# A new order of products, output steps and loads in the steady part of a convolution and SwiGLU kernel

## The chip, the core and the metric

The kernel runs on one core of a Trainium2 chip. The core has a matrix engine (TensorE, PE in the profile), a vector engine (VectorE, DVE), an engine for activations (ScalarE, ACT), a general one (GpSimd, POOL) and SyncE (SP), whose queue issues most of the transfers here. Each engine takes its instructions in order and waits on semaphores for the others. On-chip data lie in SBUF; TensorE writes to PSUM, which is held here as four double banks of 128 partitions by 1024 numbers. The metric is the device time of one execution in microseconds, from runs of the same program; a profiled execution gives the trace.

## The reference

A causal convolution of 7 taps over 8 sequences of 4096 tokens with 192 channels (8 heads share softmaxed taps), then an RMS norm and a SwiGLU feed-forward with 1536 inner channels, all in float32:

```python
out = np.einsum('hk,bskhg->bshg', w, x_unf)      # x_unf: 7 shifted copies of x
xn = x / rms * rms_g
g = xn @ w_gate
silu = g * (1.0 / (1.0 + np.exp(-g)))
val = xn @ w_val
return (silu * val @ w_out)
```

Almost all the work is three products per token, 192 x 1536 twice and 1536 x 192 once.

## The kernel before, in words

**Pairs.** The 32768 tokens are cut into 32 pairs of two groups of 512 tokens. Pair 0 and the first half of pair 1 are computed by plain products while the weights are converted. From pair 2 on every pair runs in the same way, and that is the steady part.

**Products.** The inner channels are cut into six blocks (0 to 5) of two 128-channel parts, so that a pair and a block make a 2 x 2 problem of cells a, b, c, d (group by part). Blocks 0, 2, 4 and 5 use the seven products of Strassen and Winograd (P1 to P7, with Q1 to Q4 as corrections); blocks 1 and 3 use twelve direct ones (A, B, E for each cell). A product is six matmuls of 512 columns in a split float32 format (`product`, L920). Together there are 68 a pair. Gate and value stand in the two halves of a double bank. Cells b, c and d of a Strassen block are put together from banks: f1 copies a to b, f3 copies c to SBUF, f4 and f5 add them (L991).

**Weights of the products.** The 48 pieces of weights a pair needs (192 KB each) don't fit in SBUF. They stand in DRAM (`wd`) and pass through a ring of ten slots. `ring_load` is called by the last product that uses a slot, and issues on SP's queue the load of the next piece of the list into that slot. The list is the order in which products first use the pieces, so the n-th load follows the (n-10)-th release. The c and d products of blocks 1 and 3 share three pieces: each set stays in the ring from its first to its second use. R starts the ring; its buffer is lent before that to the tokens of pair 2.

**Gates.** For each cell ScalarE makes the Silu of the gate (words ga to gd, L997) and VectorE multiplies it by the value (ma to md, L1004) into a cell of the hidden layer.

**Steps.** The output product is a 2 x 2 problem over two halves of the inner channels, again by Strassen and Winograd. For each block four sums of cells are made first (h1 to h4, L974, on VectorE or GpSimd), which overwrite cells: h2 may overwrite a cell only when step o1 of its block has read it, h4 only after o2. A step o*form.block* is one block's share of one of seven products in tiles of 32 columns (`step`, L947, 6 instructions in the program, 12 in the trace). There are 42 a pair. They gather in banks X, Y and Z; c1, c2 and s7 copy a bank on ScalarE; C22 and C21 (L1021) add two results on VectorE. o3 adds to the bank that C22 has to have read. T11, T12, T21, T22 (L962) transpose the results, and `leave` stores them (words st, ten a pair).

**Next pair.** The tokens of a later pair are loaded (ld), convolved by seven taps (cv0 on ScalarE, the others on VectorE, L455), squared, summed, scaled on GpSimd (sq, red, pow, bc, mul), put to DRAM in another layout (pl) and fetched back (ft). Four sums x1 to x4 (L842) and, for each of five operands, a split in three parts follow: n on ScalarE (L685), l on VectorE or GpSimd (L828), d on VectorE (L830).

**Order.** All of it is written out by hand. LINE is TensorE's order for one pair. ORDER is a list of words for one turn of the loop: p4 emits four entries of LINE; other words name the engine (V, A, G, S for VectorE, ScalarE, GpSimd and SP) and the operation; a plus or a minus after a word means the next pair or the one before. FIRST is the turn for pair 1. An engine runs its own words in the order given and takes no notice of how they mix with others.

Of the kernel before, what the change touches and what calls it, by code (L numbers as in the profile page):

```python
# [20 lines left out]
def kernel(  # L21
# [36 lines left out]
    PAIRS = B * NB  # L58
# [18 lines left out]
        "a5 b5 c5 d5",  # L77
    )
    ORDER = (
# [30 lines left out]
    )  # L110
    LINE = (
# [18 lines left out]
    x_sb = {}  # L130
# [31 lines left out]
    def load_part(p, h, eng):  # L162

        if h == 0:
            x_sb[p] = xs.tile([P, TB + HALO, GS], F32, name="xh")
        load_head(p, p // NB, (p % NB) * PT, h, eng)
# [219 lines left out]
    scr = {}  # L386
# [459 lines left out]
    class Pair:  # L846
# [81 lines left out]
        def step(self, form, k):  # L928
            b = ACC[form]
# [130 lines left out]
    def put_away(p, h, eng):  # L1060
        if h == 0:
            scr[p] = dram.tile([D, PT], F32, name="xd")
# [248 lines left out]
```

## Time and profile before

| what | value |
|---|---|
| runs | 2467.02 us median of 3 (2466.46 to 2467.69) |
| the profiled execution | 2466.55 us; its span 2464.8 us |
| granted TensorE clock | 0.999 |
| TensorE busy | 2449.7 us (99%) |
| VectorE busy | 2025.1 us (82%) |
| ScalarE busy | 1017.7 us (41%) |
| GpSimd busy | 835.0 us (34%) |
| DMA | 430.55 MB, mean 175 GB/s |

How to read it: busy time is the sum over which an engine had an instruction at work; the span runs from the first to the last instruction. The chain of waits follows the last instruction back, at each step to what released it. A timeline row is start, length, engine, line, operation, tiles and shapes, a count, and in brackets the idle time before it and who ended it. A window row gives for a stretch the busy time of TensorE, its weight loads, VectorE, ScalarE and GpSimd, then the granted clock, the share of the DMA engines and GB/s. Line numbers are those of the kernel before; in the changed one they are 23 or so higher.

### The profile page before, as it was taken

The numbers are of one execution on the slowest core, as the hardware profiler recorded it, in microseconds if no ns is written. First come the engines' busy times: TensorE is split into PE (matmuls) and PEld (weight loads), VectorE is DVE, ScalarE is ACT, GpSimd is POOL, SyncE is SP. The second block draws the span as 40 slices with busy tenths as digits, with TensorE's granted clock in tenths as the row PEclk, the third lists the DMA queues.
The fourth block names the chain that finished last, engine by engine and source line by source line (L and its number), as shares of the span: only waits on it lengthen the run. The fifth ranks groups of instructions, "written<-read, shape, count | busy, mean of one in ns | idle before, by whom it ended". The sixth has DMA issues, their size and how long they took to land.

```text
span 2464.8 us, 69197 instructions
## 1 busy us (share of the span) xinstructions
PE 2449.7 (99%) x29136; PEld 1892.1 (77%) x29136; DVE 2025.1 (82%) x2530; ACT 1017.7 (41%) x1431; POOL 835.0 (34%) x624
## 2 busy tenths in 40 slices
PE   8999999999999999999999999999999999999999
PEld 5647777778877777777788777777877777787777
DVE  8688878888888889888888888888887898888874
ACT  6443434433344434344334344334444343443332
POOL 0541333423343333333323334233433333333222
PEclk9999999999999999999999999999999999999999
DMA  7374678666778666676666786666786666776653
GB/s 152 61 209 133 175 179 206 185 178 164 170 196 205 175 170 171 172 204 184 194 159 176 180 210 182 177 165 170 195 205 179 165 172 173 202 187 194 159 162 95
DMA packets 716392, 430.55 MB, mean 175 GB/s; under 512 B 510330, under 2 KB 702386, under 8 KB 716082
## 3 DMA queue, kind: packets, MB, share of 16 engines
q1 hardware_dynamic: 712336, 425.21, 66.6%
q8 instruction: 230, 3.77, 0.7%
q10 hardware_dynamic: 3746, 0.92, 0.2%
q14 instruction: 80, 0.66, 0.1%
HBM read 366.96 MB, written 58.98 MB: 173 GB/s over the span
## 4 chain that ended last, share of the span: by engine, by line
PE 95%; DMA 2%; DVE 1%; SPq 1%; ACT 0%; issue 0%; POOL 0%; DVEq 0%; ACTq 0%
PE ps L920 56%; PE ps L947 36%; PE ps L1101 2%; PE ps L892 1%; DMA xb<-xd 1%; DMA ht<-in_moe_w_val_dram 0%; SPq L154 0%; DVE ht L1004 0%; DMA ring<-wd 0%; DMA x<-in_x_dram 0%; DVE ht L974 0%; SPq L238 0%; DVE part L773 0%; DMA ht<-in_moe_w_gate_dram 0%; DVE ps L991 0%
## 5 line engine op out<-in xcount | busy, mean ns | idle before, releaser
L920 PE MATMUL ps<-part,ring 64*128 64x512 f32 x12240 | 1419.3, 389 | 1.2 <-DMA ring<-wd 0.7
L920 PEld LDWEIGHTS ps<-part,ring 64*128 64x128 f32 x12240 | 1150.1, 184 | 256.7 <-issue 12.3
L997 ACT ACTIVATE tt<-ps 128x512 f32<-128x512 f32 x744 | 440.1, 600 | 716.7 <-PE ps L920 654.8
L1004 DVE TENSOR_TENSOR ht<-ps,tt 128x512 f32<-128x512 f32 x744 | 498.4, 687 | 250.7 <-ACT tt L997 248.6
L947 PE MATMUL ps<-ht,wo_sb 128*32 128x384 f32 (+2 forms) x7272 | 468.3, 380 | 0.0
L974 POOL TENSOR_TENSOR ht<-ht 128x512 f32<-128x512 f32 x180 | 271.7, 1516 | 545.5 <-PE ps L947 538.1
L947 PE MATMUL ps<-ht,x 128*32 128x256 f32 (+2 forms) x6696 | 439.3, 379 | 0.0
L947 PEld LDWEIGHTS ps<-ht,wo_sb 128*32 128x32 f32 x7272 | 325.1, 110 | 113.5 <-issue 14.8
L947 PEld LDWEIGHTS ps<-ht,x 128*32 128x32 f32 x6696 | 299.6, 110 | 89.6 <-issue 0.8
L991 DVE TENSOR_TENSOR ps<-ps,tt 128x1024 f32<-128x1024 f32 x240 | 295.9, 1233 | 54.0 <-ACT tt L685 23.7
L455 DVE SCALAR_TENSOR_TENSOR y<-xh,tp,y 128x1536 f32<-128x1536 f32 x186 | 337.0, 1812 | 0.2
L685 ACT COPY ps<-ps 128x1024 f32<-128x1024 f32 (+1 forms) x151 | 134.7, 892 | 408.8 <-PE ps L920 336.9
L974 POOL TENSOR_TENSOR hs<-ht 128x512 f32<-128x512 f32 x120 | 155.3, 1295 | 261.9 <-DVE ht L1004 261.9
L685 ACT COPY tt<-ps 128x384 f32<-128x384 f32 (+1 forms) x182 | 151.8, 834 | 217.3 <-PE ps L947 153.2
L484 POOL TENSOR_SCALAR r<-r 128x8 f32<-128x8 f32 x31 | 6.2, 199 | 499.6 <-DVE r L479 499.5
L947 PE MATMUL ps<-hs,x 128*32 128x128 f32 (+2 forms) x2232 | 161.5, 379 | 0.0
L974 DVE TENSOR_TENSOR ht<-ht 128x512 f32<-128x512 f32 x192 | 133.1, 707 | 13.7 <-PE ps L947 9.7
L947 PEld LDWEIGHTS ps<-hs,x 128*32 128x32 f32 x2232 | 106.9, 110 | 29.6
L830 DVE SCALAR_TENSOR_TENSOR part<-part,xb 128x1024 fp32r<-128x1024 f32 x87 | 120.4, 1384 | 0.0
L974 DVE TENSOR_TENSOR ht<-hs,ht 128x512 f32<-128x512 f32 x156 | 108.1, 741 | 12.3 <-PE ps L947 11.7
L828 POOL TENSOR_TENSOR part<-xb,part 128x1024 fp32r<-128x1024 f32 x29 | 69.9, 2409 | 121.8 <-PE ps L920 98.9
L505 POOL TENSOR_TENSOR xh<-y,s 128x1536 f32<-128x1536 f32 x30 | 89.9, 2998 | 14.8 <-DVE s L497 8.7
(133 smaller groups left out, 1426.8 us busy)
## 6 DMA issues: line engine op xcount, KB each, us to landing
ring<-wd SPq DMA_DIRECT2D x1440, 192.0 KB
xb<-xd SPq DMA_DIRECT2D x60, 512.0 KB
xd<-xh SPq DMA_DIRECT2D x240, 96.0 KB
xh<-in_x_dram SPq DMA_DIRECT2D x192, 105.0 KB
xb<-xd SPq DMA_DIRECT2D x60, 256.0 KB
out_dram<-o_sb SPq DMA_DIRECT2D x126, 96.0 KB
out_dram<-o_sb SPq DMA_DIRECT2D x62, 128.0 KB
wd<-part SPq DMA_DIRECT2D x5, 1152.0 KB
```

The source lines that it names most:

```text
L455: nc.vector.scalar_tensor_tensor(out=y, in0=xk, scalar=w, in1=y, op0=ALU.mult, op1=ALU.add)
L505: e.tensor_tensor(out=yn[p].rearrange("p a t -> p t a"), in0=y, in1=ss[:].rearrange("p (t o) -> p t o", o=1).to_broadcast([P, TB, GS]), op ...
L685: nc.scalar.copy(out=dst, in_=src)
L828: e.tensor_tensor(out=split_of(g, 1).bitcast(F32R), in0=src, in1=high, op=ALU.subtract)
L830: nc.vector.scalar_tensor_tensor(out=split_of(g, 2).bitcast(F32R), in0=high, scalar=1.0 + SPLIT, in1=src, op0=ALU.mult, op1=ALU.subtract,)
L920: nc.tensor.matmul(out=self.both(j, c)[:, h, :], lhsT=left[HALF[h]], rhs=right[HALF[h]], start=(first and q == 0), stop=True, skip_group_c ...
L947: nc.tensor.matmul(out=self.acc(b)[i * Q : (i + 1) * Q, at : at + n], lhsT=left, rhs=cols, start=fresh, stop=True, skip_group_check=True, ...
L974: engine[eng].tensor_tensor(out=dst, in0=a, in1=b, op=op)
L991: nc.vector.tensor_tensor(out=self.both(j, c), in0=self.both(j, "b"), in1=s5, op=ALU.add)
L997: nc.scalar.activation(out=tt[:, t, :], in_=self.both(j, c)[:, 0, :], func=AF.Silu)
L1004: nc.vector.tensor_tensor(out=self.hv(j, "abcd".index(c)), in0=self.both(j, c)[:, 1, :], in1=tt[:, t, :], op=ALU.mult,)
L1101: nc.tensor.matmul(out=bank(h, bks[h])[:], lhsT=wf[HALF[h], AT[h][k], u * NF + f, :], rhs=xb[HALF[h], g, k, :], start=(k == 0), stop=(k == ...
```

## The change

LINE, ORDER and the end of FIRST are replaced, and pair 2's turn gets a list of its own, SECOND.

- LINE: 62 products, then the steps o1.1, o1.2, o1.4, o1.0, then the last six products of block 5, then 38 steps. Before it was 68 products and 42 steps. The order of the products is another, too.
- ORDER: before, a turn begins with two products of its pair, and the six last steps of the pair before follow. Now it begins with the eight last steps of the pair before, and then come its own products. Around them other words move: x3, x4 and l.0 go from GpSimd to VectorE; h sums go to GpSimd (13 instead of 11), h4 to VectorE; all n words stand behind block 5's last Silu; taps cv1 and cv2 move a turn later; fetches stand earlier than the token loads, which are spread over the steps; stores are spread over the products.
- FIRST's end: cv1, cv2 and d.0 of pair 2 are taken out (d.0 is a word of SECOND now, behind C22, T11, T22 and T21 of pair 1), and d.4 is put in behind h4.4.
- In the code: a bank counts as fresh by its first use and not by block 0, and `load_part` and `put_away` make their tile at the first part, whichever it is. PLAIN names pair 1's steps in the order that they had.

```diff
     PLAIN = (
         "a0 b0 c0 d0 o1.0 a1 b1 c1 d1 o1.1 a2 b2 c2 d2 o1.2 a3 b3 c3 d3 o1.3 a4 b4 c4 d4 o1.4",
-        "a5 b5 c5 d5",
+        "a5 b5 c5 d5 o7.0 o7.4 o1.5 o7.3 o7.1 o7.2 o2.5 o2.0 o7.5 o6.1 o6.5 o6.0 o6.4 o6.2",
+        "o6.3 o2.3 o4.0 o4.3 o5.2 o5.3 o5.1 o4.5 o5.0 o4.4 o2.2 o4.1 o2.1 o5.4 o4.2 o5.5 o2.4",
+        "o3.3 o3.1 o3.0 o3.5 o3.2 o3.4",
     )
     ORDER = (
-        "p2 Vl.2 VC22- VT11- p3- Vd.4 VT22- VT21- Vcv3+ p3- Af1.0 Af3.0 VT12- p4 Aga.0 Vcv4+",
-        "Vf4.0 Vma.0 p2 Vcv5+ p1 Sst0.4- Sst0.2- Sst1.4- Agb.1 p5 Agc.0 Aga.1 Vmb.1 Vf5.0 p3",
-        "Vcv6+ Vma.1 Vmc.0 Agb.0 Agd.0 p2 Vmb.0 Asq+ Vmd.0 p3 Af1.2 Agc.3 Af3.2 p2 Vred+ p1",
-        "Vmc.3 p1 Vf4.2 Aga.2 Vma.2 p1 Gpow+ Vbc+ p1 Vf5.2 Gmul+ p3 Spl.0+ Agd.3 Vmd.3 p3",
-        "Spl.1+ Spl.2+ Agd.2 Agb.2 Agc.2 Vmd.2 Vmb.2 Vmc.2 Spl.3+ p6 Spl.4+ Agc.1 p1 Af1.4",
-        "Spl.5+ Spl.6+ Spl.7+ Vmc.1 p3 Agd.1 Vmd.1 p2 Af3.4 p1 Vf4.4 p4 Aga.4 Sft.0+ Sft.1+",
-        "Vma.4 Vf5.4 Agb.3 p3 Agd.4 Agc.4 Vmb.3 Vmd.4 Vmc.4 p2 Sft.2+ Sft.3+ Sst0.3- Sld.0++",
-        "Sft.4+ Sft.5+ Agb.4 Sld.1++ Sld.2++ Sst1.1- Gh1.2 Vmb.4 Gh1.1 Gh3.1 Gh1.0 p1 Sld.3++",
-        "Sst0.0- Gh3.2 Sld.4++ Sst0.1- Sld.5++ Af1.5 Sld.6++ Gh1.3 Sld.7++ p1 Af3.5 p2",
-        "Sst1.0- Sst1.2- Sst1.3- Vh1.4 Vh3.4 Vh3.0 Vf4.5 An.0+ Aga.3 p3 Vma.3 p2 Gl.0+ Gh3.3",
-        "Gx3+ Vf5.5 Aga.5 Agc.5 Vma.5 Vmc.5 p3 Vx1+ Agd.5 Agb.5 An.1+ Vx2+ p11 Vmd.5 Vh2.4",
-        "Vmb.5 Vd.0+ Vh1.5 Vh3.5 Vh2.3 Vh2.1 Vh2.5 Gx4+ Gh2.0 An.4+ Ac1 p5 Vh2.2 p1 An.3+ p4",
-        "An.2+ As7 p1 Ac2 Acv0++ Vh4.0 Vd.3+ Vd.2+ p11 Vh4.5 Vl.3+ Vh4.3 Vl.4+ Vcv1++ Vl.1+",
-        "Vcv2++ Vd.1+ p3 Gh4.1 VC21 Gh4.4 Gh4.2",
+        "VT11- p2- VC22- p3- Vh4.0- Vl.2 p1- VC21- p1- Vd.0 p1- VT22- p4 Vcv6+ VT12- VT21-",
+        "Af1.0 p2 Sst1.1- p1 Vcv3+ Agb.1 Sst0.2- Vmb.1 p2 Aga.0 Vcv5+ Af3.0 Vma.0 p5 Vf4.0",
+        "Vcv1+ Aga.1 p1 Agd.1 p2 Vma.1 Vmd.1 p2 Vf5.0 Sst1.2- Agc.0 Vmc.0 p1 Agd.0 Vcv4+ p4",
+        "Vmd.0 p1 Agc.3 Agb.0 p1 Vmc.3 Af1.2 Vmb.0 p2 Vcv2+ p2 Af3.2 Vf4.2 Aga.2 p1 Vma.2",
+        "Agc.1 Sst0.1- p1 Vmc.1 p3 Vf5.2 Asq+ Vred+ Sst0.4- Agc.2 Gpow+ p1 Gh1.1 p4 Agd.2",
+        "Sst0.0- Agb.2 Vmc.2 Vmd.2 Vmb.2 p1 Agb.3 p1 Af1.4 p1 Gh3.1 Vmb.3 p1 Vbc+ Af3.4 p1",
+        "Gmul+ Vf4.4 p1 Aga.3 p1 Gh1.0 p2 Spl.2+ Aga.4 Spl.1+ Vma.3 Spl.6+ Vma.4 p2 Agc.4",
+        "Gh3.0 Spl.5+ p1 Spl.3+ Gh1.2 Spl.0+ Vf5.4 p1 Spl.4+ p1 Agd.3 Spl.7+ Vmc.4 p2 Sft.0+",
+        "p1 Vmd.3 Agd.4 Af1.5 Sft.2+ p1 Vmd.4 p1 Gh3.2 p1 Agb.4 Af3.5 Vmb.4 p1 Vf4.5 p2 Gh1.3",
+        "p2 Aga.5 Vma.5 p2 Vf5.5 p2 Sft.5+ p1 Agc.5 p1 Gh3.3 p1 Agd.5 p2 Vmd.5 Agb.5 Gh1.4",
+        "Vmc.5 Ac1 Vmb.5 An.1+ Vh1.5 Sld.7++ p1 Gh2.2 p1 Vx1+ Vx2+ Gh3.4 p1 Sst1.4- An.0+",
+        "Gh2.1 Sld.2++ Vh2.3 p3 Vh3.5 Vx3+ Vh2.5 p1 Sft.4+ An.3+ p2 Gh2.0 Vh4.3 p1 Vx4+ Vd.1+",
+        "An.4+ p1 Sst1.3- Vd.3+ Vh4.5 p1 Sst1.0- Vh2.4 p2 Sst0.3- Sld.0++ Sld.6++ Vl.3+ p1",
+        "Vl.4+ As7 p1 Sld.1++ p2 Vh4.4 Sld.3++ An.2+ Vh4.1 p1 Ac2 p2 Vl.1+ Sld.4++ Vd.2+",
+        "Vd.4+ Vh4.2 p5 Vl.0+ p2 Sld.5++ Acv0++",
+    )
+    SECOND = (
+        "VC22- VT11- p3- Vl.2 VT22- VT21- p1- Vd.0 p2- p2 VT12- p2 Vcv6+ Af1.0 p3 Vcv3+ Agb.1",
+        "Sst0.4- Vmb.1 Sst0.2- p1 Sst1.4- p1 Aga.0 Vcv5+ Af3.0 Vma.0 p5 Vf4.0 Vcv1+ Aga.1 p1",
+        "Agd.1 p2 Vma.1 Vmd.1 p2 Vf5.0 Agc.0 Vmc.0 p1 Agd.0 Vcv4+ p4 Vmd.0 p1 Agc.3 Agb.0 p1",
+        "Vmc.3 Af1.2 Vmb.0 p2 Vcv2+ p2 Af3.2 Vf4.2 Aga.2 p1 Vma.2 Agc.1 p1 Vmc.1 p3 Vf5.2",
...
+        "Sld.3++ An.2+ Vh4.1 p1 Ac2 p2 Vl.1+ Sld.4++ Vd.2+ Vd.4+ Vh4.2 p5 Vl.0+ p2 Sld.5++",
+        "Acv0++",
     )
     FIRST = (
...
-        "p1 Vmd.5 p1 Vh1.5 p2 Ac1 Sld.3++ Vh3.5 Vh2.5 Sld.4++ Sld.5++ Sld.6++",
-        "Sld.7++ Acv0++ An.0+ An.4+ Gl.0+ Vd.0+ Vl.4+ p4 Vh4.5 p1 Vh4.0 R p1 As7 p4 p2 Ac2 p1 Vcv1++ Vcv2++ Vh4.3",
-        "p9 Vh4.2 p2 Vh4.1 p2 VC21 p1 Vh4.4",
...
+        "p2 Ac1 Sld.3++ Vh3.5 Vh2.5 Sld.4++ Sld.5++ Sld.6++ Sld.7++ Acv0++ An.0+ An.4+ Gl.0+",
+        "Vl.4+ p4 Vh4.5 p1 Vh4.0 R p1 As7 p6 Ac2 p1 Vh4.3 p9 Vh4.2 p2 Vh4.1 p2 VC21 p1 Vh4.4",
+        "Vd.4+",
     )
     LINE = (
-        "P5.0 P1.0 P2.0 Q1.0 P6.0 Ab.1 Bb.1 Eb.1 P7.0 Q2.0 Aa.1 P3.0 Ea.1 Ba.1 P4.0 Q3.0 Q4.0",
-        "P1.2 Ac.3 P5.2 Bc.3 Ec.3 P6.2 P2.2 Q1.2 Ad.3 Bd.3 P7.2 Q2.2 P3.2 Ed.3 Q3.2 Q4.2 P4.2",
-        "Ac.1 Bc.1 Ec.1 Ad.1 Bd.1 P1.4 Ed.1 P5.4 P6.4 Q1.4 Ab.3 P2.4 Bb.3 P7.4 Q2.4 P3.4 Eb.3",
-        "Q4.4 Q3.4 P4.4 P1.5 Aa.3 Ba.3 P5.5 P6.5 Ea.3 P2.5 Q1.5 P7.5 Q2.5 P3.5 Q3.5 Q4.5 P4.5",
-        "o1.0 o7.0 o1.4 o1.2 o1.3 o1.1 o7.4 o1.5 o7.3 o7.1 o7.2 o2.5 o2.0 o7.5 o6.1 o6.5 o6.0",
-        "o6.4 o6.2 o6.3 o2.3 o4.0 o4.3 o5.2 o5.3 o5.1 o4.5 o5.0 o4.4 o2.2 o4.1 o2.1 o5.4 o4.2",
-        "o5.5 o2.4 o3.3 o3.1 o3.0 o3.5 o3.2 o3.4",
+        "P1.0 Ab.1 Bb.1 Eb.1 Q1.0 P6.0 P2.0 P5.0 Aa.1 Ba.1 Ea.1 Ad.1 Bd.1 Ed.1 P7.0 Q2.0 P3.0",
+        "Ac.3 Bc.3 Q4.0 Q3.0 Ec.3 P4.0 P1.2 Ac.1 Bc.1 P5.2 P6.2 P2.2 Q1.2 Ec.1 P7.2 Q2.2 P3.2",
+        "Ab.3 Eb.3 Q4.2 Q3.2 P4.2 Bb.3 P1.4 Aa.3 Ba.3 P5.4 P6.4 Ea.3 P2.4 Q1.4 P7.4 Q2.4 P3.4",
+        "Ad.3 Bd.3 Ed.3 Q4.4 P1.5 P4.4 Q3.4 P5.5 P2.5 P6.5 Q1.5 o1.1 o1.2 o1.4 o1.0 P7.5 Q2.5",
+        "P3.5 Q4.5 Q3.5 P4.5 o1.3 o1.5 o7.0 o7.1 o6.2 o2.3 o7.4 o2.0 o7.3 o2.5 o2.2 o6.3 o2.4",
+        "o6.1 o2.1 o7.2 o7.5 o6.4 o6.5 o6.0 o4.1 o4.5 o4.0 o5.0 o5.4 o5.5 o5.2 o5.1 o5.3 o4.3",
+        "o4.4 o4.2 o3.2 o3.1 o3.3 o3.0 o3.5 o3.4",
     )
...
+            self.begun = set()
...
-            fresh = form in (1, 7) and k == 0
+            fresh = (b not in self.begun) and form in (1, 7)
+            self.begun.add(b)
...
     run([w for row in FIRST for w in row.split()], 1)
-    for w in range(2, PAIRS + 1):
+    run([w for row in SECOND for w in row.split()], 2)
+    for w in range(3, PAIRS + 1):
         run([w for row in ORDER for w in row.split()], w)
```

More of the change, by code (lines that the diff above doesn't have):

```diff
@@ L162, in load_part @@
     def load_part(p, h, eng):
-        if h == 0:
+        if p not in x_sb:
             x_sb[p] = xs.tile([P, TB + HALO, GS], F32, name="xh")
@@ L850, in __init__ @@
             self.open_half, self.turned = {}, [0, 0]
+            self.begun = set()
+            self.at = {}
             self.line = self.products()
@@ L1060, in put_away @@
     def put_away(p, h, eng):
-        if h == 0:
+        if p not in scr:
             scr[p] = dram.tile([D, PT], F32, name="xd")
```

27 rows, old and new, of tables (FIRST, SECOND) are left out of this document.

## The prediction

> **What bounds the kernel now.** I read the page's engine totals first, then the chain of waits in order of time, then the timeline of single engines where the chain changes hands.
>
> ```profile
> span 2464.8 us, 69197 instructions
> ...
> PE 2449.7 (99%) x29136; PEld 1892.1 (77%) x29136; DVE 2025.1 (82%) x2530; ACT 1017.7 (41%) x1431; POOL 835.0 (34%) x624
> ...
> PE 95%; DMA 2%; DVE 1%; SPq 1%; ACT 0%; issue 0%; POOL 0%; DVEq 0%; ACTq 0%
> ```
>
> TensorE is busy for 99% of the span and carries 95% of the chain. The change removes no matmul, so it can only move what TensorE waits for. The chain shows how one pair repeats (columns: start, length, what):
>
> ```profile
> 262.52 23.54 PE ps L947 x288
> ...
> 337.69 23.54 PE ps L947 x288
> 361.23 1.58 PE ps L920 x12
> 362.81 4.04 PE ps L947 x48
> 366.85 45.53 PE ps L920 x396
> ...
> 1310.20 23.54 PE ps L947 x288
> ...
> 1384.85 23.54 PE ps L947 x288
> ...
> 2431.37 23.54 PE ps L947 x288
> ```
>
> One pair is 36 steps (23.54 us), two products of the next pair (1.58), the six last steps (4.04) and 66 products (45.53). From 1310.20 to 1384.85 it takes 74.65 us, the shortest. Over 29 pairs, from 262.52 to 2431.37, the mean is 74.79. So all irregular waiting is 0.14 us a pair, 4.1 us in the steady part. The chain names its main source:
>
> ```profile
> 475.68 5.67 DMA xb<-xd
> 481.38 1.05 ACT part L685
> ...
> 485.04 2.35 PE ps L920 x18
> ```
>
> A token load lands late, ScalarE's rounding copy (An.0) stands for it, and the Silu behind that copy releases VectorE and then TensorE.
>
> **The change, part by part.** *TensorE.* (36+6) steps and (2+66) products become 38 steps, 62 products, 4 steps, 6 products. Both orders change four times a pair between products and steps. (1.58 + 4.04) against 2 x 0.68 + 6 x 0.65 puts such a pair of changes at 0.36 us, in both. The 0.65 is (23.54 - 4.04)/30 and the 0.68 comes from the row of 60 matmuls below. Cost: 0.
>
> *ScalarE.* The new order puts every An of the next pair behind the last Silu of block 5. A late token load no longer stops a Silu. What is late next is only the split, used a whole step block later. I take the whole 4.1 us as gained.
>
> *VectorE and GpSimd.* Two x sums and one l split move from GpSimd to VectorE; h sums go the other way, 11 to 13 on GpSimd. The timeline shows what the old mix costs:
>
> ```profile
> 1234.03 1.31 POOL L842 TENSOR_TENSOR tt<-xb 128x512 f32<-128x512 f32 x1
> ...
> 1234.52 1.37 DVE L842 TENSOR_TENSOR tt<-xb 128x512 f32<-128x512 f32 x1
> 1235.92 0.69 DVE L842 TENSOR_TENSOR tt<-tt,xb 128x512 f32<-128x512 f32 x1
> ...
> 1239.05 1.71 DVE L830 SCALAR_TENSOR_TENSOR part<-part,xb 128x1024 fp32r<-128x1024 f32 x1
> ...
> 1242.01 2.49 DVE L974 TENSOR_TENSOR ht<-hs,ht 128x512 f32<-128x512 f32 x4
> ```
>
> Beside GpSimd's x sum the same operation takes 1.37 instead of 0.69 us. Four sums in 2.49 us are 0.60 apart, so VectorE's instructions overlap by 0.09. Added: two sums (1.2) and one split (1.13). Gone: two h sums (1.2), and the slowing, 0.68 on the x sum and 0.49 on the split (1.71 against 1.22). Net about 0 per pair. The tight place is VC22, which must end before o3.2. Ahead of it on VectorE, after the last block's products, stand 14 sums (8.4 us), 8 splits (9.0), VT11 (0.56) and VC22 itself (0.55). With the last Silu and its multiplication, by these rows of the page,
>
> ```profile
> L997 ACT ACTIVATE tt<-ps 128x512 f32<-128x512 f32 x744 | 440.1, 600 | 716.7 <-PE ps L920 654.8
> L1004 DVE TENSOR_TENSOR ht<-ps,tt 128x512 f32<-128x512 f32 x744 | 498.4, 687 | 250.7 <-ACT tt L997 248.6
> ```
>
> that is 0.60 + 0.69 + 18.5 = 19.8 us after the last product. TensorE has 38 - 6 = 32 steps, 20.8 us, before o3.2. A margin of 1.0, less the hand-offs: cost 0 as long as GpSimd is out of the way. GpSimd's last four h sums wait for o1.2 and take 4 x 1.3 = 5.2 us; TensorE meanwhile does two steps, six products and then some, 5.4 us, so they end before VectorE's x sums begin. Without that cover each x sum costs 0.68.
>
> *The ring on SP's queue.* It has ten slots, loaded in the order in which slots come free. In the old line a load is released at least nine products ahead of its use (6.2 us). In the new one the three pieces of Ad.1, Bd.1, Ed.1 stay until Ac.1, Bc.1 and Ec.1, and those of Ac.3, Bc.3, Ec.3 until Ad.3, Bd.3 and Ed.3. Up to six slots are held and four go round: P2.2 and Q1.2 have five products (3.4 us), some seventeen others six (4.1 us). SP's other transfers at that place are stores, a few between the loads, of results turned long before, so nothing waits there. Later Spl.2 waits on SP for GpSimd's Gmul, with two h sums ahead of that now (2.6 us); the ring loads queued behind it have leads of nine products and more, 6.2 us, which covers that: 0.
>
> ```profile
> PE ps L920 <- DMA ring<-wd: 0.7, 2, 0.5
> ```
> ```profile
> 124.65 2.01 DMA out_dram<-o_sb
> ...
> 326.09 6.22 DMA ring<-wd
> ```
> ```profile
> 1348.20:1353.20 5.00, 5.00 (x46) 3.95 (x46) 4.50 (x6) 3.68 (x5) 0.00 (x0) 1.00 0.93 298
> ```
> ```profile
> 1340.32 6.97 PE L920 MATMUL ps<-part,ring 64*128 64x512 f32 x60
> L800 SPq DMA_DIRECT2D ring<-wd x1440: 319/381/2410, 199.7 to 2423.6; - x180
> ```
>
> With the old leads TensorE waited for the ring twice in the steady part, 0.7 us. How late a load can be: one took 6.22 us, so 2.8 late per load at worst. At best it is its transfer alone, 192 KB at 298 GB/s, 0.66 us, and never late. A gain is excluded, since nothing waits now. In between: the store at 124.65, the last of the first pair's and 32 KB by the code, took 2.01 us after its issue on a quiet queue. 160 KB more at 298 GB/s are 0.55, the issue is 0.38: 2.9 us, inside the 3.4. With one other ring load ahead it is 3.6, late by 0.17. TensorE uses a piece each 0.68 us and a piece takes 0.66, so there often is one ahead. I take 0.17 us a pair, 5.1 us for 30 pairs; nearest is the quiet row, since no token transfer stands in that stretch.
>
> The Trainium skill, "DMA: Bandwidth & Descriptors", section on the anatomy of one DMA, gives about 2.0 us fixed plus the bytes at 436 GB/s, measured on GpSimd's path. By it 192 KB land in an estimated 2.45 us and no load is late; the sum would then be without the 5.1 us. The 6.22 us row does not agree with a constant, and the run after will tell.
>
> *The start.* In the old order two products of pair 2 cover pair 1's VC22, and the split that reads the borrowed ring buffer (Vd.0) is done at 196.22.
>
> ```profile
> 196.22 1.22 DVE L830 SCALAR_TENSOR_TENSOR part<-part,ring 128x1024 fp32r<-128x1024 f32 x1
> ...
> 211.44 0.69 DVE L974 TENSOR_TENSOR ht<-ht 128x512 f32<-128x512 f32 x1 [0.67 <-PE ps L947]
> 212.04 0.55 DVE L1021 TENSOR_TENSOR tt<-ps,tt 128x384 f32<-128x384 f32 x1
> 212.51 0.64 DVE L962 STREAM_TRANSPOSE o_sb<-ps 128x256 f32<-128x256 f32 x2
> ...
> 214.18 1.15 DVE L962 STREAM_TRANSPOSE o_sb<-tt 128x256 f32<-128x256 f32 x4
> ```
> ```profile
> 196.25 3.43 POOL L828 TENSOR_TENSOR part<-ring,part 128x1024 fp32r<-128x1024 f32 x1 [12.75 <-ACT part L685]
> ```
> ```profile
> 211.32 1.65 PE L920 MATMUL ps<-part,ring 64*128 64x512 f32 x12
> 212.90 4.11 PE L947 MATMUL ps<-ht,wo_sb 128*32 128x384 f32 x72
> 216.94 1.43 PE L920 MATMUL ps<-part,ring 64*128 64x512 f32 x10
> ```
>
> In the new one Vd.4 (1.13) stands between Vh4.4 and VC22: VC22 starts at 213.2, the six steps at 213.75. Vd.0 follows VT11, VT22 and VT21 (0.47 + 0.56 + 1.06) at 215.3 and ends at 216.5. The ring's first load, which went at 199.7 behind GpSimd's 3.43, now waits for it: 216.5 + 2.9 = 219.4 for the first product. The third then starts at 220.8 instead of 216.94, and one pair of changes (0.36) that the old order has behind it is still to come: +4.2 us.
>
> *The end.*
>
> ```profile
> 2454.92 4.23 PE ps L947 x48
> ```
> ```profile
> 2455.53 1.11 DVE L962 STREAM_TRANSPOSE o_sb<-tt 128x256 f32<-128x256 f32 x4
> 2459.18 0.65 DVE L962 STREAM_TRANSPOSE o_sb<-ps 128x256 f32<-128x256 f32 x2 [2.53 <-PE ps L947]
> ```
> ```profile
> 2459.66 2.04 ACTq L1053 DMA_DIRECT2D out_dram<-o_sb  x3
> ```
>
> The old order turns the second half (VT22, VT21) before the last steps, so its five stores are out early. The new one puts VT21 behind VT12: three more stores queue on ScalarE behind the three of 2459.66, +2.0 us. VC22 has three steps as cover instead of one, 4.23 becomes 4.04: -0.2. Together +1.8.
>
> Sum against the profiled execution's own 2466.55: - 4.1 + 5.1 + 4.2 + 1.8 = 2473.6. That execution is 0.5 below the median of the runs, 2467.02, so I say 2474.
>
> **Rivals.** *The ring is in time.* For it: 2.9 against 3.4 on a quiet queue. Against: one load that took 6.22. Then 2474 - 5.1 = 2469, no change; it decides as soon as landings stay under 3.4 us. The skill's rule above says this too.
>
> *VectorE is late at VC22.* Two x sums met by GpSimd (2 x 0.68) and the hand-offs eat the margin of 1.0. At 0.7 us a pair, 30 pairs, with the ring in time: 2469 + 21 = 2490. For it: the margin is 1.0 in 20.8. Against: GpSimd's sums should be over. It decides once GpSimd runs past the last product.
>
> *Faster.* TensorE's 66 products take 45.53 us, where 66 x 0.68 are 44.9. Of the 0.6 over, half of the pair of changes explains 0.2. If the new order leaves VectorE's results ready everywhere, 0.3 a pair goes, 9 us, and with the ring in time 2469 - 9 = 2460. For it: VectorE is slowed less. Against: in block 5, the product that needs Vf5 is still the third behind P7, as before. It decides if both hold.
>
> **How the numbers follow.** Forecast 0.42 (2470 to 2482 its own range), ring in time 0.34, VectorE late 0.13, faster 0.11. The measurement can tell about 0.2%, 4.9 us, from no change: 2472 up is slower, 2462 down is faster. Of the forecast 0.07 lies within that; of the faster case 0.01. So slower 0.48, same 0.42, faster 0.10. The range reaches down to just above the faster case and up to 2488, short of most of the VectorE case.
>
> **What would show it.** Right: chain rows of 24.8 us (38 steps) and 42.7 (62 products); a total for TensorE waiting on the ring of some 5 us instead of 0.7, at P2.2 and Q1.2; no "DMA xb<-xd" ahead of a Silu; a first product of pair 2 at about 219; six stores in a row on ScalarE's queue at the end. Wrong: waits of TensorE for VectorE's L1044 (VC22), GpSimd busy during the x sums, a shortest pair well under 74.6, or ring waits near zero.

## The result, and the profile after

The changed kernel takes 2491.18 us (median of 4, 2488.85 to 2494.01), the old one beside it 2466.77 (4 runs): a ratio of 1.0099, 95% interval 1.0081 to 1.0116. It is slower, as the likeliest case said, but the loss is 24 us where 7 were predicted, and the time lies above the range, which ended at 2488. Three later groups of runs of the same kernel, each on a chip of its own, gave 2490.5, 2483.6 and 2484.7; the old kernel gave 2466.0 to 2466.8 in these four groups. So edits are compared with the changed kernel of their own group.

The page of the changed kernel, its first lines and the chain's shares by engine:

```profile
span 2486.9 us, 69139 instructions
...
PE 2458.7 (99%) x29136; PEld 1927.4 (78%) x29136; DVE 2001.7 (80%) x2557; ACT 1041.1 (42%) x1431; POOL 707.3 (28%) x597
...
PE 92%; DMA 5%; DVE 1%; SPq 1%; issue 0%; ACT 0%; POOL 0%; DVEq 0%; ACTq 0%
```

VectorE and GpSimd have less to do than before (2025.1 and 835.0), and yet the span grew by 22.1. DMA's share of the chain went from 2 to 5%. What TensorE waited for (total, times, longest, us):

```profile
PE ps L942 <- DMA ring<-wd: 8.1, 12, 1.3
PE ps L970 <- DVE tt L1044: 2.4, 1, 2.4
```

The ring was 0.7 us in two waits. The chain in order of time (start, length, what):

```profile
347.04 24.84 PE ps L970 x304
371.88 42.61 PE ps L942 x372
414.49 2.74 PE ps L970 x32
417.23 2.26 PE ps L942 x18
419.54 2.35 PE ps L942 x18
421.89 24.84 PE ps L970 x304
...
597.68 6.52 PE ps L942 x55
604.21 5.65 DMA ring<-wd
609.90 19.39 PE ps L942 x168
...
2305.01 24.84 PE ps L970 x304
...
2379.76 24.84 PE ps L970 x304
...
2454.81 24.86 PE ps L970 x304
```

A pair is 38 steps (24.84), 62 products (42.61), 4 steps (2.74), 6 products (4.66 with the change back). From 2305.01 to 2379.76 one takes 74.75, against 74.65 for the shortest old pair. The mean of the 28 pairs from 347.04 to 2454.81 is 75.28, against 74.77 for the same 28 pairs of the old kernel. At 604.21 the chain leaves TensorE after some nine products of a pair, for a ring load that took 5.65 us. The old chain had such a row too (326.09), but ring loads were 0.3% of its span; here they are 3.4%.

Three parts make up the 22.1 us. The old kernel's point that answers to 347.04 is 337.69, with the four steps (2.74) off: pair 3 comes 6.6 us later. Then 28 pairs are 14.1 longer (2107.77 against 2093.68). From 2454.81 to the end it is 32.1, with the four steps 34.8, against 33.4: 1.4. The prediction had 4.2, 1.0 (-4.1 and +5.1) and 1.8. So 13.1 of the 15.1 us that it missed lie in the 28 pairs.

### The profile page after: what moved, and what is told of

Same layout as the page of the kernel before. It is cut to its first block, busy times and chain, and to the rows that moved or that the text cites. A ratio compares the mean times of both kernels' runs of the same rounds, so it can differ in the third digit from the quotient of the medians.

```text
span 2486.9 us, 69139 instructions
## 1 busy us (share of the span) xinstructions
PE 2458.7 (99%) x29136; PEld 1927.4 (78%) x29136; DVE 2001.7 (80%) x2557; ACT 1041.1 (42%) x1431; POOL 707.3 (28%) x597
## 4 chain that ended last, share of the span: by engine, by line
PE 92%; DMA 5%; DVE 1%; SPq 1%; issue 0%; ACT 0%; POOL 0%; DVEq 0%; ACTq 0%
PE ps L942 55%; PE ps L970 34%; DMA ring<-wd 3%; PE ps L1124 2%; PE ps L914 1%; SPq L174 1%; DMA ht<-in_moe_w_val_dram 0%; DVE ht L997 0%; DMA xb<-xd 0%; DMA x<-in_x_dram 0%; DVE ht L1027 0%; SPq L258 0%; DVE part L793 0%; SPq L1087 0%; DMA ht<-in_moe_w_gate_dram 0%
## 5 line engine op out<-in xcount | busy, mean ns | idle before, releaser
L942 PEld LDWEIGHTS ps<-part,ring 64*128 64x128 f32 x12240 | 1179.5, 184 | 242.7 <-issue 25.0
L970 PE MATMUL ps<-ht,x 128*32 128x384 f32 (+2 forms) x6696 | 416.1, 379 | 0.0
L997 POOL TENSOR_TENSOR hs<-ht 128x512 f32<-128x512 f32 x150 | 194.0, 1293 | 56.5 <-DVE ht L1027 56.4
L997 POOL TENSOR_TENSOR ht<-ht 128x512 f32<-128x512 f32 x150 | 194.0, 1293 | 9.4
L997 DVE TENSOR_TENSOR ht<-ht 128x512 f32<-128x512 f32 x222 | 152.2, 697 | 10.6 <-PE ps L970 10.4
L970 PE MATMUL ps<-hs,x 128*32 128x128 f32 (+2 forms) x2232 | 130.6, 379 | 0.4 <-ACT tt L705 0.3
L997 POOL TENSOR_TENSOR ht<-hs,ht 128x512 f32<-128x512 f32 x90 | 114.5, 1287 | 29.4 <-PE ps L970 29.4
L471 ACT ACTIVATE y<-xh,tp 128x1536 f32<-128x1536 f32 x29 | 45.8, 1579 | 159.2 <-DMA xh<-in_x_dram 153.4
L848 DVE TENSOR_TENSOR part<-xb,part 128x1024 fp32r<-128x1024 f32 x87 | 105.7, 1215 | 0.0
L850 DVE SCALAR_TENSOR_TENSOR part<-part,xb 128x1024 fp32r<-128x1024 f32 x87 | 105.7, 1215 | 0.0
```

Source lines behind the costliest of these rows:

```text
L471: nc.scalar.mul(y, xk, w)
L848: e.tensor_tensor(out=split_of(g, 1).bitcast(F32R), in0=src, in1=high, op=ALU.subtract)
L850: nc.vector.scalar_tensor_tensor(out=split_of(g, 2).bitcast(F32R), in0=high, scalar=1.0 + SPLIT, in1=src, op0=ALU.mult, op1=ALU.subtract,)
L942: nc.tensor.matmul(out=self.both(j, c)[:, h, :], lhsT=left[HALF[h]], rhs=right[HALF[h]], start=(first and q == 0), stop=True, skip_group_c ...
L970: nc.tensor.matmul(out=self.acc(b)[i * Q : (i + 1) * Q, at : at + n], lhsT=left, rhs=cols, start=fresh, stop=True, skip_group_check=True, ...
L997: engine[eng].tensor_tensor(out=dst, in0=a, in1=b, op=op)
```

## The experiments

The table is worked out from the traces: the time from each product's start to the next one's, less what that place takes undisturbed (the 10th percentile over the pairs), summed over pairs 3 to 31 by the place of the product that starts late, in us. "P3.0" are the places P3.0 to P4.0; "middle" the ones from P1.2 to P3.4, where loads have leads of five to seven products; "block 5" those from Ad.3 to Q2.5; "P3.5" that place alone. "Steps" is the same for the 38 steps as a whole: what they take beyond their 10th percentile, summed over these pairs. "Pair" is the mean of the 28 pairs. The columns tell where TensorE is late; they are no prices in time, for those of the first row add up to 19.6 us, where its pairs are 14.1 longer than the old ones.

```
run                          time    P3.0  middle  block 5  P3.5  steps   pair
changed kernel              2491.2    8.3     8.1      0.5   1.3    1.4  75.28
e5_again                    2490.5    5.3    11.9      0.8   3.4    1.8  75.42
e9_ref                      2483.6    5.2     6.0      0.3   1.1    0.2  75.10
e13_ref                     2484.7    5.9     7.2      0.2   2.0    1.6  75.23
e1_stores_later             2480.0    0.0     8.5      0.4   0.3    1.6  75.00
e10_stores   (with e9)      2480.2    0.0    10.4      0.2   0.1    2.2  75.06
e2_reload                   2476.8    6.8     2.0      0.3   0.5    1.9  75.04
e11_reload   (with e9)      2477.2    3.2     1.3      0.4   0.2    0.1  74.87
e12_three    (with e9)      2470.6    0.0     1.4      0.4   0.5    0.7  74.80
e6_put_away  (with e5)      2497.7    7.3    10.1      0.4   0.0    9.2  75.56
e14_act_put  (with e13)     2500.2    3.9     7.7     14.8   0.1    1.3  75.70
e17_best                    2468.2    0.0     0.9      0.4   0.2    2.1  74.82
```

**Two stores on SP's queue.** SP's issues in one pair of the changed kernel (start, length, line, what; L820 is the ring load, L1076 a store):

```profile
598.61 3.76 SPq L820 DMA_DIRECT2D ring<-wd  x2
602.47 0.38 SPq L1076 DMA_DIRECT2D out_dram<-o_sb  x1
602.94 0.42 SPq L820 DMA_DIRECT2D ring<-wd  x1
603.41 0.70 SPq L1076 DMA_DIRECT2D out_dram<-o_sb  x1
604.21 7.01 SPq L820 DMA_DIRECT2D ring<-wd  x6
```

The load at 604.21 is P3.0's. Over all pairs it goes out 0.82 us (median) after its slot came free, because two stores stand ahead of it, and lands 4.28 us after its issue. The account to be tried is that it lands so late because those stores and the loads they held up move at the same time. It is there 0.18 us before TensorE starts its product (median), and in 13 of 30 pairs the product starts as the load lands. The edit:

```diff
-Af1.0 p2 Sst1.1- p1 Vcv3+ Agb.1 Sst0.2- Vmb.1
+Af1.0 p2 p1 Vcv3+ Agb.1 Vmb.1
-Vf5.0 Sst1.2- Agc.0
+Vf5.0 Sst1.1- Sst1.2- Agc.0
-Sst0.4- Agc.2
+Sst0.4- Sst0.2- Agc.2
```

> The changed kernel with two of the ten stores of a pair moved on SP's queue: the two that stand ahead of the loads of Q2.0 and P3.0 go where two other stores of the pair stand, some 18 and 33 products later. Theory SP: these stores delay the issue of P3.0's load by 0.82 us and the crowding behind them makes it land 4.3 us after its issue; without them the load goes out as its slot comes free, lands within 3.5 us, and the 7.9 us that TensorE loses at P3.0 over 30 pairs go: about 2483. Rival, held slots: P3.0 is late because slots are held by pieces used twice; then the wait at P3.0 stays and the time stays near 2491. Rival, crowded transfers: the five loads that follow each other there slow each other whatever stands between; then the issue delay goes, but the landing stays at 4.3 us and at most a third of the 7.9 us goes: about 2488.

2479.95 (1.0057, 1.0040 to 1.0074). This group had no changed kernel in it, so the run was made again beside one:

> The changed kernel again, as the yardstick for the next three, which run beside it on one chip: 2487 to 2493 if its two earlier groups (2491.2 and 2490.5) hold on any chip; near 2484 if the runs of the two stores, the double loads and the old start and end, which ran without it, owe a part of their gains (11, 14 and 10 us) to their chip.

> The two stores moved, as before. By the traces, what goes is the wait at P3.0: 5 to 8 us less than the changed kernel beside it, whatever the chip. If the earlier 11 us were the edit's own, 11 again.

2483.6 and 2480.2. The loads in the run with the stores moved:

```profile
524.05 11.22 SPq L820 DMA_DIRECT2D ring<-wd  x9
535.32 1.15 SPq L1076 DMA_DIRECT2D out_dram<-o_sb  x2
```

P3.0's load now goes out 0.04 us after its slot came free and lands in 2.51 us (median), 2.7 ahead of its use. The wait at P3.0 is gone in both runs (5.2 to 0.0 in the second group). The crowding was that of the stores, not of the loads among themselves, which follow each other as before. But the time fell by 3.4 us only. In its trace the stores now stand among the short leads, and the middle has 10.4 instead of 6.0; that trace is the slowest of four runs that spread from 2475.8 to 2483.4, so the size of this loss is uncertain. Against 11 us in the first group, which had no yardstick, some 7 belong to the group and not to the edit, if the edit is worth the same in both.

**The leads of five and six.** The pieces that the c and d products of blocks 1 and 3 share are loaded once for each, so that no slot is held in between:

```diff
-    pieces_of = list(dict.fromkeys((j, RIGHTS[w]) for w, j in gate_line))
...
+    TWICE = (1, 3)
+
+    def piece(w, j):
+        return j, RIGHTS[w], w[-1] if j in TWICE and w[0] in "ABE" and w[1] in "cd" else ""
+
+    pieces_of = list(dict.fromkeys(piece(w, j) for w, j in gate_line))
```

> The changed kernel with the six pieces that the products of columns c and d share in blocks 1 and 3 loaded once for each instead of held in between: 54 loads of 192 KB a pair instead of 48, and all slots go round. Theory held slots: the loads that had a lead of five and six products (P6.2, P2.2, Q1.2, P7.2, Q2.2, P6.4, Q2.4, P3.4) get nine or more; the 6.2 us that TensorE loses there go, P3.0's 7.9 us stay: about 2485. Rival, crowded transfers or a full SP queue: 12% more loads make it worse, above 2493.

> The six shared pieces loaded twice, as before. By the traces, what goes are the waits of the leads of five and six: 5 to 7 us less than the changed kernel beside it. If the earlier 14 us were the edit's own, 14 again.

2476.8 and 2477.2, the second 6.4 us under its yardstick of 2483.6. TensorE's waits for the ring as listed, of the yardstick and of this run:

```profile
PE ps L942 <- DMA ring<-wd: 5.6, 7, 1.1
```
```profile
PE ps L947 <- DMA ring<-wd: 1.9, 2, 1.1
```

The middle falls from 6.0 to 1.3 although the ring loads 12% more: not the amount of data is short there, but the time between a slot's release and its use. P3.0 stays in part (3.2), as it must, its lead being the same eight products.

**Both, with the start and the end of the old kernel.** The same edits, and the two of e3: Vd.0 of pair 2 ahead of the ring's start (R), and VT22, VT21 ahead of VT12 in the last turn alone:

```diff
-"Vl.4+ p4 Vh4.5 p1 Vh4.0 R p1 As7 ...
+"Vd.0+ Vl.4+ p4 Vh4.5 p1 Vh4.0 R p1 As7 ...
-        run([w for row in ORDER for w in row.split()], w)
+        words = [v for row in ORDER for v in row.split()]
+        if w == PAIRS:
...
+            k = words.index("VT12-")
+            words.insert(words.index("VC21-") + 1, words.pop(words.index("VT22-")))
+            words.insert(words.index("VT22-") + 1, words.pop(words.index("VT21-")))
+        run(words, w)
```

> The changed kernel with the two stores moved, the six pieces loaded twice, Vd.0 early at the start and the old end, and the put-aways left where they were. Theory: the run with all edits stayed at 2477.6 because its moved put-aways made the token load late (TensorE waits for h sums of VectorE, which stand behind work that needs the tokens: 3.8 us in the listed waits, 5.8 us of stalls among the steps in all). Without that edit the stalls fall under 2 us and the wait at P3.5 is back with up to 2 us: 2472 to 2475. Rival: those stalls come from the extra loads or the early start instead; then they stay and the time is 2478 or more.

2470.6 (10 runs; 1.0019, 1.0010 to 1.0028), 13 us under its yardstick. The two causes need both edits: with longer leads the moved stores do no harm in the middle (1.4).

**The put-aways.** Ahead of the last block's products SP issues eight transfers of normalized tokens (L1087), some between ring loads:

```profile
1612.48 1.92 SPq L1087 DMA_DIRECT2D xd<-xh  x3
1614.49 0.57 SPq L820 DMA_DIRECT2D ring<-wd  x1
1615.10 0.53 SPq L1087 DMA_DIRECT2D xd<-xh  x1
1615.73 0.55 SPq L820 DMA_DIRECT2D ring<-wd  x1
1616.33 1.19 SPq L1087 DMA_DIRECT2D xd<-xh  x2
1617.62 0.56 SPq L820 DMA_DIRECT2D ring<-wd  x1
```

An issue takes 0.53 to 0.64 us here, a ring load too, instead of 0.32 alone; a product takes 0.68. SP falls behind by 0.6 us with each put-away, and P3.5's load goes out 4.74 us (median) after its slot came free; the queue ahead of it holds it in nearly every pair, not its slot. Two edits, each for Spl.3, Spl.0, Spl.4 and Spl.7: behind the ring loads, and on ScalarE's queue.

```diff
-p1 Spl.3+ Gh1.2 Spl.0+ Vf5.4 p1 Spl.4+ p1 Agd.3 Spl.7+ Vmc.4 p2 Sft.0+
+p1 Gh1.2 Vf5.4 p1 p1 Agd.3 Vmc.4 p2 Spl.3+ Spl.0+ Spl.4+ Spl.7+ Sft.0+
or
+p1 Apl.3+ Gh1.2 Apl.0+ Vf5.4 p1 Apl.4+ p1 Agd.3 Apl.7+ Vmc.4 p2 Sft.0+
```

> The changed kernel once more, unchanged, beside the next three. If the waits for the ring are the same from one execution and chip to the next, 2491 again and 15 to 18 us of waits. If their size is a matter of the execution (how transfers fall on each other), the time moves by several us, and then only the differences within one group of runs count, and the waits of each trace.

> The changed kernel with the last four of the eight put-away transfers of normalized tokens (Spl.3, Spl.0, Spl.4, Spl.7) behind the ring loads of the last block on SP's queue instead of between them. Theory SP: the issue of the loads of P6.5 to P3.5 falls behind their slots by 1.3 to 4.7 us, because each put-away between them takes 0.6 us to issue and each load 0.55 us; with four fewer in between it falls behind by at most 2.5 us at P3.5, and the 2.9 us that TensorE loses there go: 3 us less than the changed kernel beside it. Rival: the token load that follows comes later by what the loads gain, the copy behind it holds ScalarE's As7, and the steps wait: no gain, or a loss of 1 to 3 us.

2490.5 and 2497.7: 7 us slower. P3.5's load goes out 1.4 us behind its slot instead of 4.8, and its wait went (3.4 to 0.0): the issues ahead of it on SP were its cause. The rival came true at a higher price. The second token fetch lands 0.8 us later against the steps (median), VectorE's sums stand behind work on those tokens, and TensorE waits among the steps:

```profile
PE ps L970 <- DVE ht L997: 6.0, 8, 2.1
```

> The changed kernel as the yardstick for the next three on their chip: between 2483 and 2491, as its groups so far.

> The changed kernel with four of the eight put-aways (Spl.3, Spl.0, Spl.4, Spl.7) on ScalarE's queue instead of SP's. Theory SP: what makes P3.5 late is the time that SP needs to issue them, not their data; P3.5's load falls behind its slot by 2 us instead of 4.7, its 1.6 to 4.3 us of waits go, and the token load is not later than before: 2 to 4 us less than the changed kernel beside it. Rival, data: the transfers crowd each other whichever queue issues them; the wait stays. Rival, ScalarE: four issues of about 0.6 us delay Silus of blocks 4 and 5 that TensorE waits for: more time.

2484.7 and 2500.2: 15.5 us slower. P3.5's load is 2.8 us behind its slot instead of 4.7 and its wait is gone (2.0 to 0.1). But Q1.5's load, three products earlier, now lands as its product starts in 22 of 30 pairs, and TensorE loses 14.8 us in block 5. What SP waited for, and TensorE:

```profile
SPq L820 <- DMA xd<-xh: 17.6, 24, 1.8
```
```profile
PE ps L942 <- DMA ring<-wd: 11.2, 20, 1.3
```

SP holds the ring load until a put-away has landed, a wait that the old place on its own queue did not show. The semaphores in the traces say why. Every transfer of the kernel signals one of eight semaphores, in turn over all queues, and its queue first waits until the transfer that last had this semaphore has landed. In one pair (ScalarE's put-aways, then SP's ring loads, the first of them Q1.5's):

```profile
1012.78 2.09 ACTq L1087 DMA_DIRECT2D xd<-xh  x3
```
```profile
1016.25 2.73 SPq L820 DMA_DIRECT2D ring<-wd  x4
```

The put-away of 1012.78 lands at 1016.19, and Q1.5's load, which has its semaphore, goes out behind that. In the yardstick the semaphore of this load was last a ring load's, issued 5.9 us before (median), and has long been signalled. With ScalarE issuing beside SP the turn comes round sooner: the one before is a put-away 3.5 us old, and it holds the load in 22 of the 29 pairs from pair 3 on, for 16.8 us in all. This is how the program shares its semaphores, not a fault of the second queue. The Trainium skill, "DMA: Bandwidth & Descriptors", section "Issuing engines are not separate DMA queues", says that transfers of all issuing engines interleave on the same 16 DMA engines and that another queue saves only issue time. The run agrees: issue time was saved, and the loads beside the put-aways landed no sooner (Q1.5's 3.31 us after its issue, 2.83 in the yardstick).

> The changed kernel with the edits of all the others: two stores moved, the six shared pieces loaded twice, four put-aways moved, Vd.0 early at the start, and the old end. If the causes found so far are the whole loss of the steady part: 2491.2 less 7.9 (P3.0), 6.2 (leads of five and six), 2.9 (P3.5) and 2.0 (end) = 2472, with under 2 us of waits for the ring; what is left over the old kernel is then the start (some 5 us). If another cause is hidden behind the ring, the ring's waits go and the time stays above 2477.

2477.6, 12.8 under the changed kernel of its group (2490.5). With the put-aways behind the loads the steps lose 5.6 us in pairs 3 to 31; in the run without that edit (2470.6, in another group) they lose 0.7.

> All edits that take a cause away without adding one: stores moved, pieces loaded twice, put-aways on ScalarE, start of the run before, old end. If the ring was the loss of the steady part, its waits are under 2 us and the time is 2468 to 2471, the old kernel's time but for the start. 2475 or more, if ScalarE's issues delay Silus.

2486.5, against 2484.7 for the changed kernel beside it: ScalarE's queue takes back all that the other edits bring.

**The start and the end.**

> The changed kernel with the start and the end as the old order had them: Vd.0 of pair 2 done before the ring is started, and in the last pair VT22 and VT21 behind VC21, ahead of VT12. By the trace of the changed kernel: the first product of pair 2 starts at 218.75 us; with Vd.0 early it needs only VC22 and the last steps, about 215, so -3.5; the end gives back 1.3 of the last stores. Together about 2486, with the waits in the steady part unchanged. Rival: the first product then waits for something else (the last steps behind VC22, or the split Vl.2), and less than 1.5 us come back at the start.

2481.0, without a yardstick in its group. The end is read from the trace: in this run the last steps begin at

```profile
2449.80 24.86 PE ps L970 x304
```

and the span ends at 2479.9, 30.1 us later, against 32.1 in the changed kernel: 2.0 come back. The first product of pair 2 did not move (218.80, 218.75 before), though the ring was loaded long before. TensorE's row at the start of the changed kernel, and the windows behind it in that kernel and in e9_ref (busy time of PE, PEld, DVE, ACT, POOL; then the granted clock):

```profile
213.03 5.79 PE L970 MATMUL ps<-ht,wo_sb 128*32 128x384 f32 x72 [2.40 <-DVE tt L1044]
```
```profile
214.00:217.00 3.00, 3.00 (x34) 2.26 (x30) 1.68 (x4) 0.00 (x0) 0.00 (x0) 0.51 0.10 17
```
```profile
214.00:217.00 3.00, 3.00 (x62) 2.41 (x56) 2.00 (x5) 0.00 (x0) 0.00 (x0) 1.00 0.02 5
```

After 2.40 us of waiting for VC22 the granted clock is 0.51 for three microseconds, and six steps take 5.79. So it was in e3, where nothing else held the product. In e9_ref the clock stays, and the ring's late start takes the time instead.

```diff
-"... p2 VC21 p1 Vh4.4", "Vd.4+"        SECOND: "VC22- VT11- p3- Vl.2 ...
+"Vd.0+ ... R ... p2 VC21 p1 Vh4.4"     SECOND: "VC22- VT11- Vd.4 p3- Vl.2 ...
```

> The changed kernel with the start alone changed: Vd.0 of pair 2 before the ring is started, and Vd.4 behind VC22. By the trace VC22 is then done 1.1 us earlier, the eight steps behind it and the first product of pair 2 start 1.1 us earlier, at 217.6 instead of 218.7, and the ring's first piece is there. Theory of the prediction (the start costs 4.2): 2 to 3 us less than the changed kernel beside it. Rival: pair 2 is held further on by its token load, which SP issues late; then the second block of products starts at 295.8 as before and at most 1 us is gained.

2481.7, 3.1 under its yardstick (e13_ref). TensorE in this run:

```profile
211.65 4.11 PE L969 MATMUL ps<-ht,wo_sb 128*32 128x384 f32 x72 [1.26 <-DVE tt L1043]
```

The wait is half as long, the clock stays at 1.00 (as it did in e13_ref), the first product starts at 215.7 instead of 218.9, and pair 3 begins its 38 steps 2.6 us earlier. The rival (token load of pair 2) would have left 1 at most.

**The old kernel.** Two runs try on it the 4.1 us that the prediction wanted to gain. The first moves An.0 (ScalarE's copy) and Gl.0 (GpSimd's subtraction on it) behind the gate work of block 5:

```diff
-Vh3.4 Vh3.0 Vf4.5 An.0+ Aga.3 p3 Vma.3 p2 Gl.0+ Gh3.3
+Vh3.4 Vh3.0 Vf4.5 Aga.3 p3 Vma.3 p2 Gh3.3
-Agd.5 Agb.5 An.1+ Vx2+
+Agd.5 Agb.5 An.0+ Gl.0+ An.1+ Vx2+
```

> The old kernel with one copy moved on ScalarE: An.0 of the next pair behind the last Silu of block 5 instead of ahead of the first (and the GpSimd subtraction that needs it behind it). Theory: of the 4.1 us that the old steady part loses against its shortest pair, the 3 us in five long pairs come from a Silu that stands behind this copy while the token load is late: about 2464. Rival: the late load stops the next work on VectorE and GpSimd instead (the x sums that read the same tokens), and the time stays at 2467.

2514.9, 49 us slower. The long products of the old order did get rarer (two blocks of 66 products over 45.65 us instead of five), but GpSimd's subtraction, moved with the copy, now runs beside VectorE's h sums. TensorE's wait for them in this run, then one such sum, then GpSimd at that time:

```profile
PE ps L947 <- DVE ht L974: 26.2, 58, 1.1
```
```profile
1335.36 2.41 DVE L974 TENSOR_TENSOR ht<-hs,ht 128x512 f32<-128x512 f32 x1 [1.04 <-PE ps L947]
```
```profile
1334.83 2.38 POOL L828 TENSOR_TENSOR part<-xb,part 128x1024 fp32r<-128x1024 f32 x1 [3.13 <-ACT part L685]
```

One h sum takes 2.41 us (the mean of its kind in the old kernel is 0.74), and TensorE waits for such sums 58 times. The Trainium skill, "SBUF — State Buffer", section "SBUF: two separate sides", says that a VectorE instruction with two SBUF inputs and a GpSimd instruction that reads SBUF lock the port pair that they share, and that whichever starts first holds it for its whole instruction. Here the sum ends 0.56 us after GpSimd's subtraction, which agrees.

The second brings one token fetch three products forward:

```diff
-Vf4.4 p4 Aga.4 Sft.0+ Sft.1+
+Vf4.4 p1 Sft.0+ p3 Aga.4 Sft.1+
```

> The old kernel with the first token load of the next pair issued three products earlier on SP's queue (ahead of the last ring load before it). Theory: the long pairs of the old order (46.0 us and more instead of 45.5 for the 66 products) come from the copy An.0 that stands for this load ahead of a Silu; a load that lands 1 to 2 us earlier takes away three or four of the five: 2 to 3 us less than the old kernel, about 0.1%. Rival: the load waits on SP for the last put-away to land, holds the ring loads behind it, and TensorE waits at Q1.5: no gain or a loss of 1 to 3 us.

2465.92 (11 runs) against 2466.11 (15 runs): 0.9998, 0.9989 to 1.0007. No gain that could be measured. But four blocks of 66 products still take over 45.7 us in its trace, against five in the old kernel, so the edit hardly reached what it aimed at, and the run does not show that nothing can be gained there.

**What is left.** The two stores moved, the pieces loaded twice, the old end, Vd.0 early, and VC22 ahead of Vh4.4 and of Vd.4 (the edits above, with Vh4.4 moved as well); the second run also moves four stores in pair 2's turn behind the token fetch Sft.5:

```diff
-"VC22- VT11- p3- Vl.2 ...        "... p2 VC21 p1 Vh4.4", "Vd.4+"
+"VC22- Vh4.4- VT11- Vd.4 p3- ... "Vd.0+ ... p2 VC21 p1"
-Spl.3+ Sst0.3- ... Sst1.1- Spl.7+ ... Sst0.0- Af1.5 ... Sst0.1- Vmd.4 ... Sft.5+
+Spl.3+ ... Spl.7+ ... Af1.5 ... Vmd.4 ... Sft.5+ Sst0.3- Sst1.1- Sst0.0- Sst0.1-
```

> The changed kernel with the edits that helped: two stores moved, six pieces loaded twice, old end, Vd.0 early, and at the first pair's end VC22 ahead of Vh4.4 and Vd.4 behind both. From the run of three edits (2470.6) the start of the run before takes 3 us and VC22 ahead of Vh4.4 0.7 more: 2467, the old kernel's time within what can be measured. If the start is held by the token load of pair 2, the first product comes at 215 and pair 2 loses it again: 2470.

> The same, and in the second pair four stores of the first pair's output behind the token loads on SP's queue instead of ahead of them. If the 1.8 us that TensorE loses among pair 2's steps come from a token load that SP issues late, 1 to 2 us go: 2465 to 2466. If not, the time is that of the run beside it.

2468.2 and 2467.7 (11 runs each), the old kernel 2465.7 (21): 1.0009, 1.0000 to 1.0018, both. The first of them has a span of 2466.5. The start of its first and last blocks of 38 steps, in the chain:

```profile
341.49 24.84 PE ps L974 x304
...
2436.47 24.86 PE ps L974 x304
```

28 pairs take 74.82 each, old 74.77. With the ring in time the new order is as fast as the old one, within the 0.2% that these runs can tell, and not faster. Moving four more stores of pair 2 changed nothing that can be measured (2467.7 against 2468.2), so they are not what holds that pair. What does stays open. In the chain of the first of them, the steps of pair 2 stop for a ScalarE copy that comes behind a token load:

```profile
273.67 6.46 DMA xb<-xd
280.15 1.04 ACT part L704
281.62 9.96 PE ps L974 x120
```

No version beat the old kernel.

## Why the prediction was wrong, point by point

*TensorE, 0:* right. 38 steps are 24.84 us and 62 products 42.5 to 42.6, as said; 74.75 for the shortest pair against 74.65. (62 products in 42.5 us are 0.685 each, and 66 would take 45.2: of the 0.6 us in which the rival "Faster" saw a gain, half came from rounding to 0.68.)

*ScalarE, -4.1:* wrong. With the ring's waits gone (e17) the pair is 74.82 and the old one 74.77, so nothing was gained. The step that failed is "What is late next is only the split, used a whole step block later". ScalarE's copy As7 stands behind the same copies and releases TensorE in the middle of the step block:

```profile
1635.80 6.03 DMA xb<-xd
1641.85 1.05 ACT part L705
1642.90 0.39 ACT tt L705
1643.33 9.96 PE ps L970 x120
```

Among the steps of pairs 3 to 31, 0.1 to 2.2 us are lost in the runs whose put-aways stay in place, for this copy and for other waits together. In e17 the shortest pair is 74.67 and the mean 0.15 above it, where the old kernel's mean is 0.12 above its own: the irregular loss did not go, it has other places (2.1 us among the steps, 1.5 at the ring's places). No run moved As7 alone, so its share stays open.

*VectorE and GpSimd, 0:* right.

```profile
1103.02 0.69 DVE L862 TENSOR_TENSOR tt<-xb 128x512 f32<-128x512 f32 x1
...
1120.62 0.52 DVE L1044 TENSOR_TENSOR tt<-ps,tt 128x384 f32<-128x384 f32 x1
```
```profile
1097.61 2.54 POOL L997 TENSOR_TENSOR ht<-hs,ht 128x512 f32<-128x512 f32 x2
```

GpSimd ends at 1100.2, the x sums after it take 0.69, and VC22 ends at 1121.1, 0.5 us ahead of its step. The rival "VectorE is late at VC22" did not come about; e4 shows that the contention behind it is real.

*The ring, +5.1:* the short leads do cost time, 8.1 us in this trace and 6.0 to 11.9 in its repeats, and the run that lengthens those leads gives back 6.4. That the 5.1 comes near is partly luck, for its places were wrong: P2.2 and Q1.2, with five products, land in 2.4 us (median), not in 2.9 to 3.6, and cost 0.7 us together. P7.2 and Q2.4, with leads of six products (which the sum had in time) and landings of 3.0 and 3.2 us, cost the most of them in this trace, 2.9. The step that failed is that SP's queue was put at nothing, in two sentences: "SP's other transfers at that place are stores, a few between the loads ... so nothing waits there", and for the put-aways "leads of nine products and more, 6.2 us, which covers that". Those stores wait for nothing, but each takes SP 0.4 to 0.7 us, and what follows them lands later: 5 to 8 us at P3.0, with a lead of eight products. The put-aways put the queue back by 4.7 us, not by the 2.6 of GpSimd's wait: 1 to 3 us at P3.5. The 2.45 us that the prediction works out from the Trainium skill ("DMA: Bandwidth & Descriptors", "Anatomy of one DMA — SWDGE (gpsimd) path") agrees with P2.2 and Q1.2. It does not agree with P3.0, whose 192 KB took 4.28 us, and 2.51 with the stores moved.

*The start, +4.2:* the product at 219 came (218.75). It came by the predicted way: in the chain a ring load that stood for Vd.0 leaves at 216.66 and TensorE goes on behind it. The wait of 2.40 us for VC22 and the slowed clock, which no term held, run beside that; in e9_ref, at full clock, the product comes at 218.6 as well. Undone in part, 3.1 come back. Pair 2 then lost some 2 us more to the ring and to its steps, which no term held.

*The end, +1.8:* 1.4, and 2.0 come back when it is undone.

*The sum:* the profiled execution is 2488.85, 2.3 under the median; the old one was 0.5 under its own. The same kernel differs by 7 us between groups of runs (2490.5 and 2483.6, on two chips). The loads that are just in time in one are late more often in another (P3.0 and the middle together have 11.2 us in e9_ref and 17.2 in e5_again); whether the chip or the occasion does it was not tried.

## What to carry to other kernels

A load's lead is counted from the moment its queue can issue it, not from the moment its buffer comes free: add up the issue time of everything that stands between on that queue, stores of long-finished results included. Holding a buffer for a second use shortens every other load's lead; loading the piece again was 6 us cheaper here, at 12% more ring loads. A second queue saves issue time, but where both queues share a few semaphores in turn, a transfer on one can come to wait for one on the other. An order whose waits are hidden by a few tenths of a microsecond showed different times in different groups of runs, so an edit to it needs the unedited kernel in its own group.

## What was not expected of the hardware

- A wait of TensorE of 2.4 us at the first pair's end was followed by a granted clock of 0.50 for some 3.5 us in seven of the thirteen traces that have this wait, and not in the other six. With waits of 1.26 us (e15) and none (e17) it stayed at 1.00.
- SP's issue of a ring load takes 0.32 us alone and 0.55 between put-aways.
- The landing of the same 192 KB load had medians from 2.4 to 4.3 us by its place among the products, and of 5.3 to 7.2 us, at most 8.8, for the loads issued ahead of a step block, where there is time.
- The old order gave 2465.7 to 2466.8 in six groups of runs, the new one 2483.6 to 2491.2 in four.
